# A pair's norm one unit sooner, the last w_out parts in w_in's buffers, and the first two w_in tiles in turns

## The chip, the cores and the metric

The kernel runs on one core of one Trainium2 chip. A core has a matrix engine (PE, with its weight loads shown apart as PEld), a vector engine (DVE), a scalar engine (ACT), GpSimd (POOL) and a sync engine (SP) that here issues most transfers. The metric is the time of the device for one execution, in microseconds; the kernel before took 970.9 us (median of three runs, 970.87 to 973.09). The profiled execution has a span of 971.1 us, and all times of the profile are counted from its start.

## The reference

q, k and v have the shape (8, 8, 576, 64): batch, heads, sequence, head size. The attention is linear: no softmax, one 64 x 64 matrix per head. Its normalised output is the input x of a gated MLP with 512 inputs and 2048 hidden units. The MLP's weights are float64 in memory.

```python
kv  = np.einsum('bhsd,bhse->bhde', k, v)
out = np.einsum('bhsd,bhde->bhse', q, kv)
rms = np.sqrt(np.mean(out * out, axis=-1, keepdims=True) + 1e-06)
x   = out / rms * g_norm            # -> (4608, 512)

h   = x @ w_in                      # (4608, 2048)
sp  = np.maximum(h, 0.0) + np.log1p(np.exp(-np.abs(h)))
g   = h * erf(sp)
y   = g @ w_out                     # (4608, 512)
```

## The kernel before

**Tiling.** The 4608 rows are cut into nine groups T of 512 rows. Groups 0 to 7 are the first 512 rows of each batch element; group 8 gathers the 64 rows that are left of each. The eight heads are taken as four pairs p, so one pair gives 128 of the 512 columns of x. The 2048 hidden units are 16 tiles f of 128; four tiles are a batch b. A hidden product has the shape 128 x 512 (hidden units by rows), a w_out product 128 x 512 (rows by outputs).

**A pair's attention** (`attention`, line 253) is a list of pieces that the loops place between the MLP's matmuls: `products` (kv_ps on L279, transposes of q into qt_ps on L301), `apply` (se_ps on L307, then the square on ACT, L310), `halve`, `mean` (ms_ps on L328/L329 or L333; on ACT a table load, Ln L340, Exp L341, Square L342 and a table load back), `norm` (three DVE operations, L348, L351 and L360, the last of which writes a quarter of x) and `split` (x cut into a high part on ACT, L385, and a low part and a sum of both on DVE, L388 and L389). Where the caller names no banks, kv_ps, qt_ps, se_ps and ms_ps share the two PSUM banks of `ps_at`: L348 is the last reader of ms_ps, L360 that of se_ps.

**First stage: groups 0 and 1** (loop at line 569). They are computed in plain fp32 (`h_ps`, L592, four matmuls of 128x512 over c = 0 to 3; `o_ps`, L471), one unit n for each group and f, while DVE and ACT convert the float64 weights. A conversion has three steps: `load_w`, `w_split` (L195 and L204 on DVE, L203 and L207 on ACT) and `w_join` (L214, L218, L228 on DVE). `w_order` lists the tiles by the unit at which they are due; the function `weights` does the split of the next tile, the join of the present one and the load of a later one. Four raw tiles are in memory at a time (`RAW`). The pieces of group 0's four pairs run ahead of the loop, with conversion steps between them as `w_rounds` says, and in the loop those of the next group's pairs: `pieces_of` puts the products of pair p at f = 3(p+1), its norm at f = 3(p+1)+3. A unit's work on DVE comes in this order: the norm that is due, the weights that are due, the multiplication by the erf.

**Main stage: groups 2 to 8** (loop at line 684). The weights have been cut into three parts each and stored in DRAM (`w_kept`), and `load_parts` fetches them again for each group: 768 KB a tile, w_in's into four buffers (`w_in_p`), w_out's into seven (`w_out_p`). One pass m of the loop is four hidden products of batch m (`hidden`: eight n_ps and four m_ps matmuls each, L434) and four w_out products of batch m-1 (`result`, j = 0 to 3, also twelve matmuls). `product` rotates through six banks in pairs. `FETCH` says which part is fetched at which place of a pass. Each pass also carries one pair of the next group, and the tuple `places` says after which of the eight products its pieces stand: 1 to 4 stand behind a hidden product, 5 to 8 behind a w_out product. The pieces are products, apply, halve, mean, norm, split:

```python
        places = (0, 2, 3, 5, 7, 8)
        if T + 1 == B:
            places = (0, 0, 0, 5, 7, 7)
        elif T + 2 == B and b == NB - 1:
            places = (0, 2, 3, 5, 7, 7)
```

So the norm stands behind w_out product j=2, whose two sums (L414 and L419 into e) DVE does first. Behind j=1 stands the multiplication of h by the erf (L745). [...] the order above is written out by hand (`manual_schedule`), and the tile pools add the waits for buffers.

Of the kernel before, what the change touches and what calls it, by code (L numbers as in the profile page):

```python
# [39 lines left out]
FP32 = mybir.dt.float32  # L40
# [10 lines left out]
BATCH = 4  # L51
# [7 lines left out]
def kernel(  # L59
# [11 lines left out]
    P = 128  # L71
# [3 lines left out]
    G = J * P  # L75
    R = S - G
    NP = H // 2
    KC = DM // P
    FC = DF // P
# [71 lines left out]
    w_in_sb = first_w.tile([P, KC, DF], FP32, name="w_in_sb")  # L151
# [58 lines left out]
    def w_join(which, f, k):  # L210
# [18 lines left out]


    w_order = sorted(
        [(0, "in", 0, 1), (1, "in", 1, 1)]
        + [(f, "in", f, 2) for f in range(2, FC, 2)]
        + [(min(f + LAG, (f + FC) // 2 + 1), "out", f, 2) for f in range(0, FC, 2)]
    )
    w_at = {"load": 0, "split": 0, "join": 0}
# [7 lines left out]
    def weights():  # L244

        w_next("split")
        w_next("join")
        w_next("load")
# [254 lines left out]
    for _ in range(2):  # L503
# [7 lines left out]
        2: ("join", "load", "split"),  # L511
        3: ("join", "load"),
        5: ("split",),
        6: ("join", "load"),
    }
    banks_0 = {"kv_ps": (ps_at, "at"), "qt_ps": (ps_h, "h"), "ms_ps": (ps_h, "h")}
    first = [attention(0, p, banks_0 | {"se_ps": (ps_o, f"o{p}")}) for p in range(NP)]
# [19 lines left out]

    def load_parts(which, n):

        pool = w_in_p if which == "in" else w_out_p  # L540
        for _ in range(n):
            if w_seq[which]:
                key = w_seq[which].pop(0)
                t = pool.tile([P, 3, G], FP32, name=f"w_{which}_parts", tag="w")
                nc.sync.dma_start(out=t, in_=w_kept[key])
                w_now.setdefault(key, []).append(t)


    def pieces_of(T):


        steps = [([], []) for _ in range(FC)]
        for p in range(NP):
            products, apply, halve, mean, norm, split = attention(T, p)
            short = T < FIRST or p == NP - 1
            f = (BATCH - 1) * (p + 1) if T < FIRST else BATCH * p
            steps[f][1].append(products)
            steps[f + 1][1].append(apply)
            steps[f + 2][0].append(halve)
            with_erf = short and (f + 2) % BATCH == BATCH - 1  # L560
            steps[f + 3 - short][short].append(partial(mean, table=not with_erf))
            steps[f + 4 - short][0].append(norm)
            steps[f + 5 - 2 * short][0].append(split)
        return steps

    to_cut = [(which, f) for which in ("in", "out") for f in range(FC)]
    hs, ss = {}, {}
    whole = FIRST * FC - BATCH
    for n in range(FIRST * FC + 1):
        T, f = divmod(n, FC)  # L570
        if n == FC:
            early_room.close()
            late = ctx.enter_context(tc.tile_pool(name="late", bufs=1))
            x_new = ctx.enter_context(tc.tile_pool(name="x_new", bufs=1))
            acc = ctx.enter_context(tc.tile_pool(name="acc", bufs=J))
            stage_room = ctx.enter_context(ExitStack())
            stage = stage_room.enter_context(tc.tile_pool(name="stage", bufs=5))
            x_forms[FIRST] = late.tile([P, 3, KC, G], FP32R, name="x_forms0")
        if T < FIRST:
            if f == 0:  # L580
                steps = pieces_of(T + 1)
            for piece in steps[f][0]:
                piece()
        while w_at["join"] < len(w_order) and w_order[w_at["join"]][0] <= n + 2:
            weights()
        done = n - LAG + 1
        if 0 <= done < whole:
            nc.vector.tensor_tensor(out=hs[done], in0=hs[done], in1=ss[done], op=ALU.mult)
        if T < FIRST:
            h_ps = ps_h.tile([P, G], FP32, name="h_ps", tag="h")  # L590
            for c in range(KC):
                nc.tensor.matmul(  # L592
                    h_ps,
                    lhsT=w_in_sb[:, c, f * P : f * P + P],
                    rhs=xT[T][:, c, :],
                    start=(c == 0),
                    stop=(c == KC - 1),
                )
            if n == whole:
                old_h = wide.tile([P, BATCH, G], FP32, name="h", tag="h")  # L600
            h = hs[n] = old_h[:, n - whole] if n >= whole else unit("h_sb")
            s = ss[n] = unit("s_sb")
            nc.scalar.copy(h, h_ps)
            nc.scalar.activation(s, h, AF.Softplus)
            for key in list(w_new):
                w_lower(*key)
            if T == FIRST - 1:
                for key in to_cut[:2]:
                    w_upper(*key)
                if not w_new and stage_room is not None:  # L610
                    stage_room.close()
                    stage_room = None
                    w_in_p = ctx.enter_context(tc.tile_pool(name="w_in_p", bufs=BATCH))
                    load_parts("in", BATCH)
            if n == 0:
                w_next("split")
            for piece in steps[f][1]:
                piece()
            if f % BATCH == BATCH - 1:
                for i in range(n - BATCH + 1, n + 1):  # L620
                    nc.scalar.activation(ss[i], ss[i], AF.Erf)
                softplus_table()
            if T == FIRST - 1:
                for key in to_cut[2:3]:
                    w_upper(*key)
                del to_cut[:3]
        if n >= LAG:
            T2, f2 = divmod(n - LAG, FC)
            last = n - LAG in (FC - 1, whole - 1)
            project(f2, hs[n - LAG], last)  # L630
            if last:
                sums()
                if T2 == 0:
                    for j in range(J):
                        store(T2, j, es.pop(j))
# [48 lines left out]
    for m in range(first_batch, batches + 1):  # L684
        T, b = divmod(m, NB)
        todo = []
        if T + 1 < NG:
            todo = list(attention(T + 1, b))
            if b == 0:
                side = late_r if T % 2 == FIRST % 2 else late  # L690
                x_forms[T + 1] = side.tile([P, 3, KC, G], FP32R, name=f"x_forms{(T + 1) % 2}")

        def piece():
            if todo:
                todo.pop(0)()

        places = (0, 2, 3, 5, 7, 8)
        if T + 1 == B:
            places = (0, 0, 0, 5, 7, 7)
        elif T + 2 == B and b == NB - 1:  # L700
            places = (0, 2, 3, 5, 7, 7)

        def pieces(place):
            while todo and places[-len(todo)] <= place:
                todo.pop(0)()

        def fetch(place):
            for which in FETCH[place].split():
                load_parts(which, 1)

        pieces(0)
        g, done = g_next, len(g_next)
        g_next = []
        if m < batches:
            h = wide.tile([P, BATCH, G], FP32, name="h", tag="h")
            s = gate_r.tile([P, BATCH, G], FP32, name="s", tag="s")
        for i in range(BATCH):
            if m < batches:
                n_ps, m_ps = hidden(T, b * BATCH + i)
            fetch(i)  # L720
            if i == 0:
                for half in range(done, 2):
                    g.append(cut_upper(old_h, half))
            if done <= i < 2:
                cut_lower(old_h, i, g[i])
            if m < batches:
                nc.scalar.activation(h[:, i], n_ps, AF.Copy, scale=SHIFT - 1.0)  # L727
                add(h[:, i], m_ps)
                nc.scalar.activation(s[:, i], h[:, i], AF.Softplus)  # L729
            pieces(i + 1)  # L730
        if m < batches:
            for i in range(2):
                nc.scalar.activation(part(s, i), part(s, i), AF.Erf)  # L733
            if len(todo) < 3:
                softplus_table()
        T2, b2 = divmod(m - 1, NB)
        w = [w_now["out", b2 * BATCH + f].pop(0).bitcast(FP32R) for f in range(BATCH)]
        for j in range(J):
            result(T2, b2, j, g, w)
            fetch(BATCH + j)  # L740
            if j == 1 and m == batches - 1:
                cut_lower(h, 0, g_next[0])

            for half in range(2) if j == 1 and m < batches - 1 else (j,) if j < 2 and m == batches - 1 else ():
                nc.vector.tensor_tensor(  # L745
                    out=part(h, half), in0=part(h, half), in1=part(s, half), op=ALU.mult
                )
            if j == 0 and m == batches - 1:
                g_next.append(cut_upper(h, 0))
            pieces(BATCH + 1 + j)  # L750
        old_h = h
# [33 lines left out]
```

## Time and profile before

| what | value |
|---|---|
| time, median of three runs | 970.9 us |
| span of the profiled execution | 971.1 us |
| first stage (until the main loop's first matmuls) | about 268.6 us |
| main loop, groups 2 to 6: DVE busy | 400.05 of 508 us |
| main loop, groups 2 to 6: DMA engines' share, GB/s | 0.83, 295 |
| from 34 to 60 us: DVE, ACT busy | 25.76 and 22.02 of 26 us |
| critical chain, PE's share | 81% |

In a row of the timeline stand the start, the duration, the engine and line, the operation with output and inputs, the shape and the count; in brackets the idle time before it and what released it. In a row of the page's group table stand busy time and mean duration, then the idle time ahead of the group and what ended most of it. A row such as "m_ps x4" holds four matmuls in a row. PE's start of a matmul is observed; its end is longer than the distance to the next one, since matmuls overlap.

### The profile page before, as it was taken

What the parts mean: (1) busy time and instruction counts of PE and PEld (TensorE: products, weight loads), DVE (VectorE), ACT (ScalarE), POOL (GpSimd) and SP (SyncE); (2) the same over time, 40 slices, a digit from 0 to 9 for tenths busy, and PEclk for the clock granted to TensorE, in tenths of its full rate; (3) what the DMA queues carried; (4) which work ended last, traced back from release to release, by engine and by line L of the source; (5) the groups of instructions that cost most, each with busy time, mean ns of one, the idle gap of its engine ahead of it and who ended that gap; (6) DMA issues with size and microseconds to landing.
All of it is one profiled execution on the core that took longest, in us unless ns stands there. A gap on an engine that the chain in (4) does not pass through costs nothing.

```text
span 971.1 us, 11732 instructions
## 1 busy us (share of the span) xinstructions
PE 944.2 (97%) x4328; PEld 677.5 (70%) x4328; DVE 728.4 (75%) x1031; ACT 615.2 (63%) x821; POOL 2.4 (0%) x10
## 2 busy tenths in 40 slices
PE   6899999999999999999999999999999999999997
PEld 4344444444477877787778777877887787878885
DVE  3987866766377777887787778877777777887666
ACT  3888865686576666666666666666666666665551
POOL 0000000000000000000000000000000000000000
PEclk9999999999999999999999999999999999999999
DMA  9855506879289975998789877987796669767852
GB/s 281 246 177 178 179 1 272 311 320 361 95 293 352 378 272 210 306 367 295 247 270 357 305 274 243 350 290 294 247 335 254 259 228 363 275 261 295 351 231 76
DMA packets 100937, 259.76 MB, mean 267 GB/s; under 512 B 44049, under 2 KB 57361, under 8 KB 100881
## 3 DMA queue, kind: packets, MB, share of 16 engines
q1 hardware_dynamic: 99248, 256.73, 74.0%
q10 hardware_dynamic: 1568, 2.29, 0.8%
q8 instruction: 34, 0.56, 0.2%
q14 instruction: 23, 0.18, 0.1%
q0 software_dynamic: 64, 0.00, 0.0%
HBM read 224.40 MB, written 34.60 MB: 267 GB/s over the span
## 4 chain that ended last, share of the span: by engine, by line
PE 81%; DVE 12%; ACT 4%; DMA 2%; issue 1%; SPq 0%; DVEq 0%
PE n_ps L434 35%; PE m_ps L434 18%; PE h_ps L592 10%; PE o_ps L471 9%; PE se_ps L307 3%; DVE h L745 3%; DVE e L419 2%; PE qt_ps L301 2%; PE kv_ps L279 2%; DMA w_out_parts<-w_out 1%; DVE x L360 1%; DVE e L414 1%; DVE u L351 1%; DVE u L348 1%; PE ms_ps L328 1%
## 5 line engine op out<-in xcount | busy, mean ns | idle before, releaser
L434 PE MATMUL n_ps<-x_forms,w_in_parts 128*128 128x512 f32 x896 | 233.3, 402 | 1.7 <-ACT x_forms L385 1.2
L434 PE MATMUL n_ps<-w_out_parts,g_forms 128*128 128x512 f32 x928 | 231.8, 391 | 2.5 <-DMA w_out_parts<-w_out 2.5
L434 PEld LDWEIGHTS n_ps<-w_out_parts,g_forms 128*128 128x128 f32 x928 | 174.1, 188 | 41.7 <-DMA w_out_parts<-w_out 3.4
L434 PEld LDWEIGHTS n_ps<-x_forms,w_in_parts 128*128 128x128 f32 x896 | 166.8, 188 | 45.8 <-issue 9.6
L729 ACT ACTIVATE s<-h 128x512 f32<-128x512 f32 x112 | 71.0, 634 | 168.0 <-DVE h L419 168.0
L434 PE MATMUL m_ps<-w_out_parts,g_forms 128*128 128x512 f32 x464 | 124.2, 389 | 0.0
L434 PE MATMUL m_ps<-x_forms,w_in_parts 128*128 128x512 f32 x448 | 120.1, 390 | 0.0
L419 DVE TENSOR_TENSOR h<-m_ps,h 128x512 f32<-128x512 f32 x112 | 77.1, 688 | 56.9 <-ACT h L727 41.5
L592 PE MATMUL h_ps<-xT,w_in_sb 128*128 128x512 f32 x256 | 116.7, 600 | 2.9 <-DVE xT L360 2.0
L471 PE MATMUL o_ps<-w_out_sb,h_sb 128*128 128x512 f32 x224 | 100.5, 592 | 0.0
L434 PEld LDWEIGHTS m_ps<-w_out_parts,g_forms 128*128 128x128 f32 x464 | 87.1, 188 | 18.1
L414 DVE SCALAR_TENSOR_TENSOR e<-n_ps,e 128x512 f32<-128x512 f32 x88 | 60.5, 687 | 49.2 <-PE n_ps L434 49.2
L434 PEld LDWEIGHTS m_ps<-x_forms,w_in_parts 128*128 128x128 f32 x448 | 84.1, 188 | 17.6
L419 DVE TENSOR_TENSOR e<-m_ps,e 128x512 f32<-128x512 f32 x116 | 80.3, 692 | 18.5 <-PE m_ps L434 12.2
L592 PEld LDWEIGHTS h_ps<-xT,w_in_sb 128*128 128x128 f32 x256 | 49.0, 192 | 64.3 <-issue 58.0
L471 PEld LDWEIGHTS o_ps<-w_out_sb,h_sb 128*128 128x128 f32 x224 | 42.0, 190 | 49.8 <-issue 48.3
L389 DVE SCALAR_TENSOR_TENSOR g_forms<-g_forms 128x1024 fp32r<-128x1024 f32 x58 | 71.1, 1225 | 2.0
L388 DVE TENSOR_TENSOR g_forms<-h,g_forms 128x1024 fp32r<-128x1024 f32 x58 | 70.6, 1218 | 1.5 <-ACT g_forms L385 1.2
L727 ACT ACTIVATE h<-n_ps 128x512 f32<-128x512 f32 x112 | 65.5, 585 | 4.1 <-PE n_ps L434 4.1
L385 ACT ACTIVATE g_forms<-h 128x1024 fp32r<-128x1024 f32 x58 | 58.9, 1059 | 13.8 <-PE m_ps L434 11.0
L745 DVE TENSOR_TENSOR h<-h,s 128x1024 f32<-128x1024 f32 x56 | 66.0, 1219 | 0.4 <-ACT s L733 0.4
L385 ACT ACTIVATE x_forms<-x 128x512 fp32r<-128x512 f32 x28 | 17.7, 631 | 66.8 <-DVE x L360 66.8
(84 smaller groups left out, 981.2 us busy)
## 6 DMA issues: line engine op xcount, KB each, us to landing
w_out_parts<-w_out SPq DMA_DIRECT2D x116, 768.0 KB, 7.6
w_in_parts<-w_in SPq DMA_DIRECT2D x112, 768.0 KB, 6.6
w_in<-w_new SPq DMA_DIRECT2D x16, 768.0 KB, 5.6
w_out<-w_new SPq DMA_DIRECT2D x16, 768.0 KB, 6.4
k_sb<-in_k_dram SPq DMA_DIRECT2D x29, 288.0 KB, 5.6
v_sb<-in_v_dram SPq DMA_DIRECT2D x29, 288.0 KB, 5.5
q_sb<-in_q_dram SPq DMA_DIRECT2D x32, 256.0 KB, 5.6
w_raw<-in_moe_w_out_dram SPq DMA_DIRECT2D x8, 1024.0 KB, 5.0
```

The lines of the kernel that those rows point to most:

```text
L307: nc.tensor.matmul(o_ps, lhsT=bd, rhs=qT, start=True, stop=True)
L385: nc.scalar.activation(high, x, AF.Copy, scale=1.0 + 2.0**-13)
L388: nc.vector.tensor_tensor(out=low, in0=x, in1=high.bitcast(FP32), op=ALU.subtract)
L389: nc.vector.scalar_tensor_tensor(out=both, in0=low.bitcast(FP32), scalar=SHIFT, in1=high.bitcast(FP32), op0=ALU.mult, op1=ALU.add,)
L414: nc.vector.scalar_tensor_tensor(out=out_, in0=ps, scalar=scale, in1=out_, op0=ALU.mult, op1=ALU.add)
L419: nc.vector.tensor_tensor(out=out_, in0=ps, in1=out_, op=ALU.add)
L434: nc.tensor.matmul(ps, lhsT=weights(form, k), rhs=moving(form, k), start=(form == forms[0] and k == 0), stop=(form == forms[-1] and k == 3),)
L471: nc.tensor.matmul(o_ps[j], lhsT=g[:, j * P : j * P + P], rhs=w_out_sb[:, f, :], start=(f == 0), stop=last,)
L592: nc.tensor.matmul(h_ps, lhsT=w_in_sb[:, c, f * P : f * P + P], rhs=xT[T][:, c, :], start=(c == 0), stop=(c == KC - 1),)
L727: nc.scalar.activation(h[:, i], n_ps, AF.Copy, scale=SHIFT - 1.0)
L729: nc.scalar.activation(s[:, i], h[:, i], AF.Softplus)
L745: nc.vector.tensor_tensor(out=part(h, half), in0=part(h, half), in1=part(s, half), op=ALU.mult)
```

## The change

It has four parts. In the main loop a pair's norm moves from place 7 to place 6, ahead of the sums of w_out product j=2. The last four w_out parts are fetched into w_in's buffers, which are no longer needed then, so that they don't have to wait for w_out buffers that are still read. In the first stage, where two weight tiles are due in one unit, one is converted ahead of the unit's pieces. And the first two w_in tiles take the blocks c of x in turns (tile 0 and tile 1 with c=0, then both with c=1, and so on), in banks of other pools, so that the PE has more to do while the last pair of x is computed; the w_in tiles up to f=3 are converted one by one instead of in twos for it.

```diff
     w_order = sorted(
-        [(0, "in", 0, 1), (1, "in", 1, 1)]
-        + [(f, "in", f, 2) for f in range(2, FC, 2)]
+        [(f, "in", f, 1) for f in range(4)]
+        + [(f, "in", f, 2) for f in range(4, FC, 2)]
         + [(min(f + LAG, (f + FC) // 2 + 1), "out", f, 2) for f in range(0, FC, 2)]
     )
...
-        6: ("join", "load"),
+        6: ("split", "join", "load", "join", "load"),
     }
...
     def load_parts(which, n):

-        pool = w_in_p if which == "in" else w_out_p
+
+        pool = w_out_p if which == "out" and len(w_seq["out"]) > BATCH else w_in_p
...
+    def due(k):
+
+        i = w_at["join"] + k
+        return i < len(w_order) and w_order[i][0] <= n + 2
+
     for n in range(FIRST * FC + 1):
...
+            if due(1):
+                weights()
             for piece in steps[f][0]:
                 piece()
-        while w_at["join"] < len(w_order) and w_order[w_at["join"]][0] <= n + 2:
+        while due(0):
             weights()
...
         if T < FIRST:
-            h_ps = ps_h.tile([P, G], FP32, name="h_ps", tag="h")
-            for c in range(KC):
+
+            if n > 1:
+                plain[n] = ps_h.tile([P, G], FP32, name="h_ps", tag="h")
+                blocks = [(n, c) for c in range(KC)]
+            elif n == 0:
+                for i, (pool, tag) in enumerate(((ps_at, "at"), (ps_o, "o0"))):
+                    plain[i] = pool.tile([P, G], FP32, name="h_ps", tag=tag)
+                blocks = [(i, c) for c in range(KC - 1) for i in range(2)] + [(0, KC - 1)]
+            else:
+                blocks = [(1, KC - 1)]
+            for i, c in blocks:
                 nc.tensor.matmul(
-                    h_ps,
-                    lhsT=w_in_sb[:, c, f * P : f * P + P],
+                    plain[i],
+                    lhsT=w_in_sb[:, c, i % FC * P : i % FC * P + P],
                     rhs=xT[T][:, c, :],
                     start=(c == 0),
                     stop=(c == KC - 1),
                 )
+            h_ps = plain.pop(n)
...
-        places = (0, 2, 3, 5, 7, 8)
+
+        places = (0, 2, 3, 5, 6, 8)
         if T + 1 == B:
-            places = (0, 0, 0, 5, 7, 7)
+            places = (0, 0, 0, 5, 6, 7)
         elif T + 2 == B and b == NB - 1:
-            places = (0, 2, 3, 5, 7, 7)
+            places = (0, 2, 3, 5, 6, 7)
```

More of the change, by code (lines that the diff above doesn't have):

```diff
@@ L566 @@
     to_cut = [(which, f) for which in ("in", "out") for f in range(FC)]
-    hs, ss = {}, {}
+    hs, ss, plain = {}, {}, {}
     whole = FIRST * FC - BATCH
+    def due(k):
+        i = w_at["join"] + k
+        return i < len(w_order) and w_order[i][0] <= n + 2
     for n in range(FIRST * FC + 1):
```

## The prediction

> **What bounds the kernel now.** I read the engine totals first, then the PE's idle gaps in order of time, and only then the other engines around each gap. Totals and the largest PE row of the page:
>
> ```profile
> PE 944.2 (97%) x4328; PEld 677.5 (70%) x4328; DVE 728.4 (75%) x1031; ACT 615.2 (63%) x821; POOL 2.4 (0%) x10
> L434 PE MATMUL n_ps<-x_forms,w_in_parts 128*128 128x512 f32 x896 | 233.3, 402 | 1.7 <-ACT x_forms L385 1.2
> ```
>
> The PE is the bound: of 971.1 us only 27 are not busy, so each part of the change is worth the PE gap it closes. The ends of PE records are modelled, so I measure a gap by distances between starts, not by the bracketed idle time (eight n_ps matmuls advance 1.81 us, the four m_ps ones 0.91, eight fp32 ones 3.43). The PE timeline holds these gaps, all that matter:
>
> ```profile
> 29.31 2.84 PE L592 MATMUL h_ps<-xT,w_in_sb 128*128 128x512 f32 x6 [0.94 <-DVE qT L348]
> 34.14 13.12 PE L592 MATMUL h_ps<-xT,w_in_sb 128*128 128x512 f32 x26 [1.98 <-DVE xT L360]
> ...
> 58.01 1.12 PE L333 MATMUL ms_ps<-qT,mean_w 128*128 128x512 f32 x2 [1.25 <-ACT qT L310]
> ...
> 123.84 0.43 PE L306 MATMUL kv_ps<-qT_last,bd_kv 128*128 128x64 f32 x2 [1.48 <-DVE bd_kv L294]
> ...
> 343.94 0.92 PE L279 MATMUL kv_ps<-v_sb,k_sb 96*64 96x64 f32 x24
> 345.13 0.66 PE L301 MATMUL qt_ps<-ident,q_sb 128*128 128x128 f32 x4 [0.27 <-DVE x L360]
> ...
> 774.02 0.49 PE L434 MATMUL n_ps<-x_forms,w_in_parts 128*128 128x512 f32 x1 [0.42 <-ACT x_forms L385]
> ...
> 956.82 0.72 PE L434 MATMUL n_ps<-w_out_parts,g_forms 128*128 128x512 f32 x2 [2.06 <-DMA w_out_parts<-w_out]
> 957.38 1.09 PE L434 MATMUL m_ps<-w_out_parts,g_forms 128*128 128x512 f32 x4
> ```
>
> The reader is to see five kinds: the start, one wait on ACT at 58, one on DVE at 124, a small one that recurs at every seam between two batches, and the last w_out part.
>
> [...] the four-matmul gap doubles from 34.14, where the clock record has 3.41 us at 0.5 and the 3.41 us before were busy for only 1.4. [...]
>
> **Part 1, the norm at place 6 instead of 7 (main loop).** Nothing is added; three DVE operations move ahead of the two sums of w_out product j=2. One seam of before, from the DVE and ACT timelines:
>
> ```profile
> 340.23 0.63 ACT L342 ACTIVATE u<-rms_r 128x512 f32<-128x512 f32 x1
> 341.49 0.68 DVE L414 SCALAR_TENSOR_TENSOR e<-n_ps,e 128x512 f32<-128x512 f32 x1
> 342.28 0.69 DVE L419 TENSOR_TENSOR e<-m_ps,e 128x512 f32<-128x512 f32 x1
> 342.88 0.68 DVE L348 SCALAR_TENSOR_TENSOR u<-ms_ps,u 128x512 f32<-128x512 f32 x1
> 343.60 0.69 DVE L351 SCALAR_TENSOR_TENSOR u<-u,rms_r 128x512 f32<-128x512 f32 x1
> 344.33 0.75 DVE L360 SCALAR_TENSOR_TENSOR x<-se_ps,gm_col,u 128x512 f32<-128x512 f32 x1
> ```
>
> The next pair's kv_ps takes the bank that L348 frees (342.88+0.68 = 343.56, and the PE's loads start only then), its qt_ps the bank that L360 frees (345.08). Put first, the norm would start at 341.5: u is ready at 340.86, 0.6 us before, so no wait is put in its place. L360 then ends at 343.7, before kv_ps begins. The sums of j=2 end 2.1 us later, near 345.0; their banks are next wanted by hidden unit 1 at 348.4. The sums of j=3 keep their time, since DVE does the same work without a gap.
>
> Price: the batches that start with odd p advance 25.21 us from kv_ps to kv_ps, those with even p 25.16. Free of waits, from the first batch at 268.6 (24.96, less 0.09 at its end), they would take 24.70 and 24.87 (the odd lack one transpose of 0.17). So 0.51 and 0.29 each. Ten odd ones give 5.0. Of nine even ones, five give 1.45. The other four open a new group T: there the low third of x (L388) still comes after j=3's sums at an unchanged time (372.27 at the first such seam, where the PE would want it at 372.0), so I leave them 0.09 each, 0.35. Sum **6.8**. The ends: 0 if those waits return elsewhere, 8.0 if all nineteen are won.
>
> Two seams without products. At 772.08 the PE takes 3.01 us to the m_ps at 775.09 instead of 1.81; with norm and split each a unit sooner, L388 would end near 773.9 where 773.67 is wanted: 0.95 of the 1.2 is won. At 864.62 the loss is 1.55, and there ACT's L342 ends only at 863.96, so the norm can't start sooner; j=2's sums now stand between it and L388, which ends 0.6 later. In the group before, the new order lets DVE wait for ACT (up to 1.7 us a batch), in others it saves 0.45, so I take **-0.4** (ends 0 and -1.5). Net +0.55.
>
> **Part 2, the last four w_out parts in w_in's buffers.** The stop at 956.82 costs 957.38-953.24-1.81 = 2.33 us: of seven w_out buffers four are read until 953, so the eighth transfer starts then and lands after the row's
>
> ```profile
> 952.75 4.03 DMA w_out_parts<-w_out
> ```
>
> of the critical chain. The four w_in buffers come free with the last hidden units, 934 to 942.4, so all four parts land near 950 at the 7.6 us from issue to landing that the page has. Nothing else waits in that queue but stores that come later. The work then met is DVE's L389 (ends 958.5), wanted by j=2 only at about 960.5. **+2.3** (ends 1.5, 2.4).
>
> **Part 3, conversion ahead of the norm where two are due.** That happens in unit n=12 only. DVE there waited 3.73 us for ACT (L342, until 110.95), and was then late with bd_kv at 123.34. With 4.8 us of conversion put into that wait the norm begins at 112.0, one us later, and bd_kv is done near 121.4; the PE wants it at 122.36. The gap of **1.5** goes (ends 0, 1.5).
>
> **Part 4, the first two tiles in turns, w_in in single tiles to f=3.** The PE's 0.94 at 29.31 goes (h_ps leaves ps_h, whose bank waited for L348) and the 1.98 at 34.14 is filled: six blocks of 0.86 from 28.15, the seventh when the last xT comes (about 33.5, since a shorter split stands before it). But DVE has no gap from 30 to 60, so converting the tiles sets what follows. Two single joins of 1.93 take 0.33 more than one double (34.00 to 37.53), and the split for f=4 moves from 37.53 to about 37.95. ACT, held by it at 38.25 (1.3 us idle), goes from 38.7; it then wins back the 0.69 that it waited for the PE at units 2, 3 and qt_ps, and reaches
>
> ```profile
> 57.38 0.58 ACT L310 ACTIVATE qT<-se_ps 128x512 f32<-128x512 f32 x1
> ```
>
> 0.25 us sooner. That L310 releases the ms_ps at 58.01, behind which all later PE work queues. So of the PE's four us only **+0.25** arrives; the rest becomes idle time before 57.8, some 3.6 us in one piece (units 4 and 5 done at 54.15). [...] I take **-1.1**. Net -0.85 (ends -1.5 and +4, if ACT isn't the limit).
>
> The stop at 808.81 (0.75 by starts) I leave as it is, +-0.5.
>
> **Sum.** 6.8+0.55+2.3+1.5-0.85 = 10.3; 970.9-10.3 = **960.6**.
>
> **The rivals.** (a) The seams keep half: L388 or the banks stop the PE a little later than now. For: DVE is 79% busy from 264 to 772 (400 of 508 us). Against: it waits 2.6 us a batch for the PE. 6.8 becomes 3: about 964.4. Chance 0.17. (b) The start is won in full (+4 instead of -0.85): 955.8. Against it stands the gapless DVE. 0.08. (c) Transfers become the limit once batches are shorter, and the seam gap turns into one for parts: only 2.3+1.5-0.85 and 0.55 remain, 967.4. Against: the DMA engines are at 83%, and parts are waited for in two places only. 0.05. (d) The norm blocks DVE on u in most batches, holding j=2's banks: if each of 28 batches lost 0.2 us instead of gaining, with part 4 at -1.5, parts 2 and 3 at 2.3 and 0: 970.9+5.6+1.5-2.3 = 975.7, slower. Against: 0.6 us of slack on u. 0.04. The forecast keeps 0.66.
>
> **Range.** The forecast's unknown ends (part 4, new groups, the 808 stop) span about 957.5 to 963; (a) reaches 965. So 957.2 to 965.0, leaving out (b) to (d) and some tail. Faster by over 0.3% means under 968.0: the forecast, (a), (b) and most of (c), 0.94; same 0.02; slower 0.04.
>
> **What would show it.** Right: no qt_ps row with a wait for L360 in the main loop, odd batches at 24.7 us and even at 24.9; waits for x_forms at new groups; no stop at the last w_out part; none at unit 13; L360 no longer before h_ps at the start, but a longer wait for L310 before ms_ps and perhaps a half-clock window after it. Wrong: DVE idle before L348 for u in batches before 772, or ms_ps near 54.

## The result, and the profile after

The changed kernel takes 966.34 us (median of four runs, 965.56 to 966.64) beside 972.0 us for the kernel before on the same chip: a ratio of 0.9939 with a 95% interval of 0.9918 to 0.9959, 5.9 us of 972. That is the direction of the forecast, but a little over half of its 10.3 us, and 1.3 us above the end of its range. The profiled span went from 971.1 to 964.5 us.

The page's totals and the row of the hidden products, after:

```profile
PE 942.4 (98%) x4328; PEld 677.5 (70%) x4328; DVE 727.9 (75%) x1036; ACT 615.4 (64%) x823; POOL 2.4 (0%) x10
L434 PE MATMUL n_ps<-x_forms,w_in_parts 128*128 128x512 f32 x896 | 234.1, 402 | 2.4 <-ACT x_forms L385 1.4
```

The PE is still the bound, but the idle time ahead of the hidden products has grown from 1.7 to 2.4 us. Nearly all of it stands at group 8's start (1.42 and 0.83 us, below), where a loss of 0.4 us was forecast. The PE timeline, with the places of before (start, duration, operation, idle time before it and who ended it):

```profile
28.11 7.38 PE L610 MATMUL h_ps<-xT,w_in_sb 128*128 128x512 f32 x16
36.10 7.13 PE L610 MATMUL h_ps<-xT,w_in_sb 128*128 128x512 f32 x16 [0.61 <-DVE w_in_sb L228]
...
49.51 0.44 PE L306 MATMUL kv_ps<-qT_last,bd_kv 128*128 128x64 f32 x2 [1.30 <-DVE qT_last L297]
...
57.14 2.07 PE L333 MATMUL ms_ps<-qT,mean_w 128*128 128x512 f32 x2 [2.85 <-ACT qT L310]
59.01 5.74 PE L471 MATMUL o_ps<-w_out_sb,h_sb 128*128 128x512 f32 x8
64.59 3.60 PE L610 MATMUL h_ps<-xT,w_in_sb 128*128 128x512 f32 x8
...
124.40 0.33 PE L306 MATMUL kv_ps<-qT_last,bd_kv 128*128 128x64 f32 x2
...
342.81 1.07 PE L434 MATMUL m_ps<-w_out_parts,g_forms 128*128 128x512 f32 x4
343.81 0.92 PE L279 MATMUL kv_ps<-v_sb,k_sb 96*64 96x64 f32 x24
344.66 0.66 PE L301 MATMUL qt_ps<-ident,q_sb 128*128 128x128 f32 x4
345.08 2.10 PE L434 MATMUL n_ps<-x_forms,w_in_parts 128*128 128x512 f32 x8
...
859.25 1.52 PE L434 MATMUL n_ps<-x_forms,w_in_parts 128*128 128x512 f32 x6
862.18 0.50 PE L434 MATMUL n_ps<-x_forms,w_in_parts 128*128 128x512 f32 x1 [1.42 <-ACT x_forms L385]
863.52 0.51 PE L434 MATMUL n_ps<-x_forms,w_in_parts 128*128 128x512 f32 x1 [0.83 <-DVE x_forms L388]
863.86 1.07 PE L434 MATMUL m_ps<-x_forms,w_in_parts 128*128 128x512 f32 x4
...
949.09 1.98 PE L434 MATMUL n_ps<-w_out_parts,g_forms 128*128 128x512 f32 x8
950.90 1.07 PE L434 MATMUL m_ps<-w_out_parts,g_forms 128*128 128x512 f32 x4
```

What the reader is to see: the two stops at the start of h_ps are down to one of 0.61 (a new one of 1.30 stands at 49.51), and none is left at unit 13 (124.40), at qt_ps or at the last w_out part (949.09). But behind the wait at 57.14 eight o_ps matmuls take 5.6 us from start to start where they took 3.43, and the first product of group 8 (859.25) takes 4.61 us to its m_ps, against 3.36 before and 1.81 when nothing stops it.

Split into stages by the starts of kv_ps, before and after: up to the main loop 268.61 and 269.06 (0.45 later); the main loop from there to the last pair's kv_ps 478.40 and 474.18 (4.22 won); from there to the end 224.1 and 221.3 (2.8 won). The last is made of 2.33 at the last w_out part, 0.79 at group 7's start (3.01 becomes 2.22), 0.75 at the stop of 808, which isn't there in this run, and -1.25 at group 8's start; 0.2 are left over, the last pair's own seam among them. The 0.75 is luck: no part of the change aims at that stop.

### The profile page after: what moved, and what is told of

Same layout as the page of the kernel before. It is cut to its first block, busy times and chain, and to the rows that moved or that the text cites. A ratio compares the mean times of both kernels' runs of the same rounds, so it can differ in the third digit from the quotient of the medians.

```text
span 964.5 us, 11755 instructions
## 1 busy us (share of the span) xinstructions
PE 942.4 (98%) x4328; PEld 677.5 (70%) x4328; DVE 727.9 (75%) x1036; ACT 615.4 (64%) x823; POOL 2.4 (0%) x10
## 4 chain that ended last, share of the span: by engine, by line
PE 84%; DVE 6%; ACT 6%; DMA 1%; issue 1%; SPq 0%; DVEq 0%
PE n_ps L434 37%; PE m_ps L434 19%; PE o_ps L471 10%; PE h_ps L610 9%; PE se_ps L307 3%; PE kv_ps L279 2%; PE qt_ps L301 1%; DVE h L419 1%; ACT s L753 1%; DMA v_sb<-in_v_dram 1%; ACT s L749 1%; DVE e L419 1%; DVE g_forms L388 1%; DMA q_last<-in_q_dram 1%; PE ms_ps L328 1%
## 5 line engine op out<-in xcount | busy, mean ns | idle before, releaser
L471 PE MATMUL o_ps<-w_out_sb,h_sb 128*128 128x512 f32 x224 | 102.7, 603 | 0.0
L414 DVE SCALAR_TENSOR_TENSOR e<-n_ps,e 128x512 f32<-128x512 f32 x88 | 60.4, 686 | 44.1 <-PE n_ps L434 44.1
L388 DVE TENSOR_TENSOR g_forms<-h,g_forms 128x1024 fp32r<-128x1024 f32 x58 | 70.6, 1218 | 1.5 <-ACT g_forms L385 1.2
```

The costliest lines, as they stand in the source:

```text
L388: nc.vector.tensor_tensor(out=low, in0=x, in1=high.bitcast(FP32), op=ALU.subtract)
L414: nc.vector.scalar_tensor_tensor(out=out_, in0=ps, scalar=scale, in1=out_, op0=ALU.mult, op1=ALU.add)
L471: nc.tensor.matmul(o_ps[j], lhsT=g[:, j * P : j * P + P], rhs=w_out_sb[:, f, :], start=(f == 0), stop=last,)
```

## The experiments

Two theories stood against each other for the first stage. Theory C (clock): part 4 moves idle time into one piece ahead of ms_ps, and the PE then runs the work behind it at half clock. Rival: the start's gain is real, and the loss lies elsewhere. For group 8's start: the norm's place against ACT's lateness. Each time below is given with the kernel before on the same chip.

**e1: without part 4.**

```diff
-        [(f, "in", f, 1) for f in range(4)]
-        + [(f, "in", f, 2) for f in range(4, FC, 2)]
+        [(0, "in", 0, 1), (1, "in", 1, 1)]
+        + [(f, "in", f, 2) for f in range(2, FC, 2)]
...
-        6: ("split", "join", "load", "join", "load"),
+        6: ("join", "load"),
...
-            if n > 1:
-                plain[n] = ps_h.tile([P, G], FP32, name="h_ps", tag="h")
-                blocks = [(n, c) for c in range(KC)]
...
-            for i, c in blocks:
+            h_ps = ps_h.tile([P, G], FP32, name="h_ps", tag="h")
+            for c in range(KC):
```

> The changed kernel without part 4 (no turns, w_in tiles in twos as before); parts 1 to 3 stay. Theory: part 4 costs about 2 us, since the PE, idle before the ms_ps of group 1's first pair, falls to half clock [...]. Then this kernel has no half-clock stretch after 57 us, keeps part 3's 1.5 us, and takes 8 to 8.5 us less than before, 2.5 us less than the changed kernel. Rival: the start's gain is real and the loss lies elsewhere; then this kernel is 0.9 us slower than the changed one, about 4.8 us less than before.

Measured: 964.25 us beside 972.25, ratio 0.9918 (0.9902 to 0.9933), 8.0 us less. The main loop begins at 265.25 instead of 269.06; 0.28 of that is an earlier start of this run (the last ms_ps of group 0 is at 26.89, in the changed kernel at 27.17). So without part 4 the first stage is 3.5 us shorter, more than the 2 us of the expectation: ms_ps comes at 56.39, 29.50 us behind that last ms_ps of group 0, and in the changed kernel 29.97. Against this run part 4 did not even bring it forward. In the profiled run of before the distance was 30.74; the section on the prediction comes back to this. The end of e1 gave something back, though. The stretches of e1 around group 8's start (columns: stretch, length, busy time and instructions of PE, PEld, DVE, ACT and POOL, granted PE clock, share of the DMA engines, GB/s):

```profile
857.00:861.00 4.00, 1.65 (x5) 0.87 (x4) 3.83 (x6) 3.01 (x4) 0.00 (x0) 0.85 0.48 187
861.00:868.00 7.00, 7.00 (x21) 5.45 (x20) 6.83 (x9) 1.83 (x3) 0.00 (x0) 0.60 0.31 112
```

There the stop for x_forms (1.52 and 0.83 us) leaves the PE busy for 1.65 of 4 us, and the clock is at half from 859.78 to 866.61: the same kind of fall at another place.

**e2: part 4 alone** (the norm's places and the pool for w_out as before, no conversion ahead of the unit's pieces).

> The kernel before with part 4 alone. Theory: ms_ps starts 0.9 us sooner (57.1), then half clock costs about 3.1 us, so the PE is some 2.1 us late at unit 13, where DVE's lateness (the 1.48 us wait for bd_kv) is now covered: the main loop begins 0.5 to 1.0 us later than before, time +0.5 to +1.0 us. Rival, the clock isn't the cause: -0.9 us.

Measured: 974.13 us beside 972.25, ratio 1.0019 (1.0011 to 1.0027): 1.8 us slower. The sign is Theory C's, the size larger (the interval, 1.1 to 2.6 us, lies above the expected 0.5 to 1.0). In its trace ms_ps starts at 57.16, the clock from 57 to 64 is 0.76 (in the changed kernel 0.55), and the wait for bd_kv in unit 13 is still 1.44 us: DVE's lateness moved along with the PE, so nothing was covered. That part of the expectation was wrong.

**e3: unit 5 done twice in the changed kernel.**

```diff
+            if n == LAG:
+                blocks = blocks * 2
             for i, c in blocks:
```

> The changed kernel with the four h_ps matmuls of unit 5 done twice (the second time over the first): 3.4 us of PE work more, put into the idle time before ms_ps. Theory of the clock: ms_ps starts near 57.6 instead of 57.1, but at full rate, and the stretch to unit 6 takes 4.4 us instead of 7.5: 2.6 us less than the changed kernel, 8 to 8.5 us less than before, although it computes more. Rival, the slow stretch has another cause (data, banks, DMA): 0.4 us slower than the changed kernel.

Measured: 964.25 us beside 972.25, ratio 0.9923 (0.9906 to 0.9939): 7.5 us less than before with 3.4 us of PE work more. The stretches of the changed kernel and of e3:

```profile
57.00:64.00 7.00, 6.86 (x9) 2.91 (x10) 3.66 (x5) 6.86 (x10) 0.00 (x0) 0.55 0.50 181
```

```profile
58.00:65.00 7.00, 7.00 (x18) 3.09 (x17) 3.69 (x5) 6.86 (x9) 0.00 (x0) 1.00 0.48 163
```

In seven microseconds the PE did 9 instructions at a clock of 0.55, and 18 at full clock; from ms_ps to unit 6 the first takes 7.45 us, the second 4.29. The two kernels differ in the repeated matmuls alone, which fill the PE's idle time. This shows Theory C for the first stage. The time moves with the clock from run to run, too: three of e3's six runs have a mean clock of 1.000 and take 962.94 to 963.26 us, the other three 0.998 and 965.23 to 967.16. The profiled one is of the second kind, with half clock behind group 8's start (861.64 to 865.06).

**e4: the first w_out product ahead of ms_ps in the changed kernel.**

```diff
+            if n == LAG:
+                project(0, hs[0], False)
             for piece in steps[f][1]:
                 piece()
...
-        if n >= LAG:
+        if n > LAG:
```

> The changed kernel with the first w_out product (unit 0's, eight fp32 matmuls, 3.43 us) ahead of the ms_ps of group 1's first pair instead of behind it. Theory: the idle 2.85 us are filled with work that has to be done anyway, the clock stays full, and the PE reaches unit 6 near 59.1 instead of 64.6: about 5 us less than the changed kernel at that point; of it 1 us may be lost to the pair's norm, which starts 1 us later on DVE: 9.5 to 10.5 us less than before. Rival, DVE and ACT set the time there: 1 us or less is won against the changed kernel.

Measured: 964.5 us beside 972.25, ratio 0.9919 (0.9905 to 0.9933): 7.9 us less, where 9.5 to 10.5 was expected. Unit 6 starts at 58.75, but then the pair's norm is waited for, as the rival had it in part:

```profile
57.89 1.02 PE L333 MATMUL ms_ps<-qT,mean_w 128*128 128x512 f32 x2
58.75 3.60 PE L610 MATMUL h_ps<-xT,w_in_sb 128*128 128x512 f32 x8
63.80 0.92 PE L279 MATMUL kv_ps<-v_sb,k_sb 96*64 96x64 f32 x24 [1.46 <-DVE qT L348]
65.32 0.66 PE L301 MATMUL qt_ps<-ident,q_sb 128*128 128x128 f32 x4 [0.59 <-DVE xT L360]
```

Unit 6 comes 5.8 us sooner than in the changed kernel, 0.5 of it by an earlier start (26.68 against 27.17 for the last ms_ps of group 0); 2.05 of the rest come back as this wait, and the main loop begins at 265.40. Part of the shortfall goes with the clock: the two runs at a mean clock of 1.000, the profiled one among them, take 962.57 and 963.32 us, the four at 0.998 or 0.996 take 964.39 to 965.47.

**e5: the norm of group 8's pairs back at place 7.**

```diff
         if T + 1 == B:
-            places = (0, 0, 0, 5, 6, 7)
+            places = (0, 0, 0, 5, 7, 7)
```

> The changed kernel, with the norm of group 8's pairs back at place 7 (the tuple for T + 1 == B is (0, 0, 0, 5, 7, 7) again). Theory: at place 6 DVE waits there for ACT's L342 and then does two sums before L388, so the first product of group 8 comes 2.8 us late instead of 1.55, [...]. Then that stop is 1.3 us shorter, no half-clock stretch follows it, and the time is 1.3 to 3 us less than the changed kernel's, 7 to 9 us less than before. Rival: ACT's lateness is what counts there, and the place doesn't matter: within 0.5 us of the changed kernel.

Measured: 963.38 us beside 972.63, ratio 0.9912 (0.9899 to 0.9924): 8.6 us less, inside the expected 7 to 9. In its trace the first product of group 8 takes 857.33 to 860.85, 3.52 us, with a stop of 0.93 for ACT and 0.23 for DVE, and the clock stays at 1.00 from 857 to 868. The place matters: 1.09 us less than the 4.61 of the changed kernel. The rest of the difference between the two includes the clock near 57, at half for 3.41 us in this run and for 6.83 in the other: from ms_ps to unit 6 it is 6.09 us against 7.45.

**e6: part 1 alone.**

> The kernel before with part 1 alone (norm at place 6). Theory from the seams counted again: odd batches 24.84 instead of 25.21 us, even ones 24.96 instead of 25.16, those that open a group unchanged: 4.3 us up to the last of them, then +0.8 at group 7's start and -1.25 (more with the half clock) at group 8's: 3.0 to 4.5 us less than before. Rival, as predicted: 6.8 and 0.55, 7.3 us less.

Measured: 969.08 us beside 972.63, ratio 0.997 (0.9961 to 0.9978), 2.9 us less. That is just under the expected 3.0 to 4.5, and far from the rival's 7.3. The seams are as in the changed kernel (24.84 and 24.96 us, 25.2 where a group opens). What else it shows is the spread: 22 runs from 967.2 to 972.8 us, and the profiled one is the slowest. Its stretches behind the stop at group 8's start and behind the last w_out part:

```profile
864.00:868.00 4.00, 4.00 (x11) 3.19 (x12) 3.86 (x5) 0.99 (x2) 0.00 (x0) 0.59 0.13 15
...
956.00:960.00 4.00, 4.00 (x12) 3.11 (x12) 1.66 (x3) 0.00 (x0) 0.00 (x0) 0.57 0.21 52
```

Both stops were followed by half clock in this execution, and in the profiled run of the kernel before neither was (1.00 from 868 to 872 and from 957 to 961). Each costs up to 1.7 us, an estimate: half of the 3.41 us that the clock record has at half.

**e7: part 2 alone.**

> The kernel before with part 2 alone (last four w_out parts in w_in's buffers). Theory: the stop of 2.3 us at the last w_out product goes, and in runs where that stop is followed by half clock up to 1.7 us more: 2.0 to 3.5 us less than before. Rival, the end is set by DVE's forms or the stores: under 1 us.

Measured: 968.73 us beside 972.63, ratio 0.997 (0.996 to 0.9981), 2.9 us less, with an interval of 1.8 to 3.9: the stop's 2.3, and perhaps some of the clock behind it. Of the four profiled kernels that keep this stop, e2 and e6 show a clock of 0.57 over four microseconds behind it, e9 shows four m_ps matmuls in 1.71 us instead of 0.91, and before shows 1.00. There is no stop left in e7's last products.

**e8: parts 1 to 3 with two places mended.** To e1 come e5's edit and

```diff
-        elif T + 2 == B and b == NB - 1:
+        elif b == NB - 1:
             places = (0, 2, 3, 5, 6, 7)
```

> Without part 4, with parts 1 to 3, and two places mended: norm at place 7 for group 8's pairs, and at each last batch of a group the split at place 7 instead of 8, ahead of j=3's sums. Theory: against the kernel without part 4 (8 us less than before) the four seams that open groups 3 to 6 win 0.2 to 0.35 us each, 1.1 us, and group 8's start 1.3 us and its half clock: 10.5 to 12 us less than before, faster than both kernels. Rival for the seams: L388 is held by ACT or x, and they stay at 25.2 us.

Measured: 961.94 us beside 972.63, ratio 0.9892 (0.9876 to 0.9907), 10.5 us less. One seam that opens a group, in the changed kernel on DVE, then in e8 on DVE and on the PE:

```profile
370.49 0.69 DVE L419 TENSOR_TENSOR e<-m_ps,e 128x512 f32<-128x512 f32 x1
371.10 0.68 DVE L388 TENSOR_TENSOR x_forms<-x,x_forms 128x512 fp32r<-128x512 f32 x1
```

```profile
367.31 0.68 DVE L388 TENSOR_TENSOR x_forms<-x,x_forms 128x512 fp32r<-128x512 f32 x1
368.02 0.69 DVE L389 SCALAR_TENSOR_TENSOR x_forms<-x_forms 128x512 fp32r<-128x512 f32 x1
368.63 0.68 DVE L414 SCALAR_TENSOR_TENSOR e<-n_ps,e 128x512 f32<-128x512 f32 x1
...
367.63 2.10 PE L434 MATMUL n_ps<-x_forms,w_in_parts 128*128 128x512 f32 x8
369.57 1.07 PE L434 MATMUL m_ps<-x_forms,w_in_parts 128*128 128x512 f32 x4
```

In the changed kernel L388 ends at 371.78, 1.76 us after n_ps has begun (370.02), which then takes 2.16 us to its m_ps; in e8 it ends at 367.99, and n_ps takes 1.94. All batches that open a group become 24.96 us instead of 25.2.

**e9: part 3 alone.**

> The kernel before with part 3 alone (one weight tile ahead of the norm in unit 12). Theory, as predicted: the wait for bd_kv in unit 13 goes, the PE gains 1.5 us there and keeps it: 1.5 us less than before. Rival: the wait is passed on to a later unit (the norm comes 1 us later): 0.5 us or less.

Measured: 972.12 us beside 973.05, ratio 0.9989 (0.998 to 0.9997), 1.1 us less. The wait in unit 13 is gone (kv_ps follows unit 13's h_ps at 122.04 without a stop, bd_kv is written at 120.93), and it isn't passed on: from unit 6 to the main loop the profiled runs that have part 3 and o_ps in its old place take 204.5 us, those without part 3 206.2. In this run the stop near 808 is 1.64 us by its idle time, 0.47 in the first run of before; over the runs of this study it goes from none to 1.64, and I have no cause for that.

**e10: the changed kernel without part 3.**

```diff
-            if due(1):
-                weights()
```

> The changed kernel without part 3. If the gains of parts 3 and 4 add, it is 1.5 us slower than the changed kernel. Theory: with part 4 the PE comes to unit 13 about 2 us late; the run with part 4 alone still showed a wait of 1.44 us for bd_kv there, so DVE's lateness moves along with the PE (its chain begins with the norm, which waits for ACT and so for the PE's ms_ps), and the two parts add: 1.2 to 1.6 us slower than the changed kernel, about 5 us less than before. Rival: covered, within 0.3 us of the changed kernel.

Measured: 967.75 us beside 973.05, ratio 0.9942 (0.993 to 0.9955), 5.6 us less. The trace has the wait for bd_kv back (1.49 us at 125.83), and from unit 6 to the main loop it takes 206.22 us against 204.47 in the changed kernel, so the parts do add there. The times can't tell: this run was at half clock for 3.41 us near 58 and the changed kernel for 6.83, which makes 1.4 us between ms_ps and unit 6 (6.09 against 7.45). By time the run is inconclusive.

**e11: e8's mended places, with part 4 and e4's edit.**

> The mended kernel (norm and split as in e8) with part 4 kept and the first w_out product put ahead of ms_ps. Theory: the main loop begins near 265.4 as in e4, against 266.7 in e8, and all seams are as in e8: 1 us less than e8, 11.5 us less than before. Rival: the wait for the pair's norm at 63.8 (1.46 and 0.59 us in e4) takes it back: equal to e8 within 0.5 us.

Measured: 960.96 us beside 973.05, ratio 0.988 (0.9864 to 0.9896), 11.7 us less: the fastest kernel of the study by its median. Its main loop begins at 266.18, e8's at 266.66; the interval overlaps with e8's, so whether part 4 is worth keeping once the PE is kept busy stays open.

## Why the prediction was wrong

It was wrong in size. In the profiled pair 6.6 us are won of the 10.3: the seams bring 2.6 less than forecast, part 4 costs 1.4 more (2.3: 0.77 won and 3.06 lost, both below) and group 8's start 0.85 more, while the stop of 808 gave 0.75 that was not in the forecast. The parts alone (e6, e7, e9 and e2) add up to 5.1 us, the whole to 5.9, so, as far as their intervals tell, the shortfall lies within the parts and not in how they act together. By the runs:

**The seams (6.8 forecast, 4.2 measured).** The mechanism held: qt_ps waits for L360 no more, the norm begins at once behind the multiplication by the erf (L348 at 341.36, with L414 of j=2 behind it at 343.47), no wait for u took its place, L388 held the seams that open a group. The step that failed is the price of a seam free of waits. I took 0.09 us ahead of kv_ps off the 24.96 us of the first batch, as a wait for L348, and left 0.06 behind qt_ps out. Neither is a wait. In all 19 seams kv_ps starts 1.00 us after the m_ps ahead of it (0.91 between products), before, when L348 ended 0.38 us ahead of kv_ps, and after, when it ended 1.77 us ahead. At the main loop's first kv_ps (269.06), 7.3 us behind the last norm, sixteen o_ps matmuls take 6.96 us instead of twice 3.43, the same 0.09 more. From qt_ps to n_ps the changed kernel takes 0.41 to 0.42 us in odd batches and 0.36 in even ones. So odd batches are 24.84 at best, not 24.70, and even ones 24.96, not 24.87. Ten by 0.37 and five by 0.20 are 4.7, less 0.37 for the last seam, which lies outside the stage, and less than 0.1 that the four opening seams lost. (In the forecast's own sum ten times 0.51 is 5.1, not 5.0, and all nineteen seams would be 7.7, not 8.0.)

**Part 4 (a loss of 0.85 us forecast, 1.8 measured by e2).** The reasoning by DVE held: the split for f=4 came at 37.89 (37.95 forecast), and L310 set ms_ps. Two steps failed, both on the clock. The first is that ACT "wins back the 0.69 that it waited for the PE". Those waits were there because the PE ran at half clock from 34.73 to 38.14 in that run of before, and I had taken this stretch to be hidden. ACT's way from the split for f=4 (L203) to L310 takes 19.13 us there, 17.90 in the changed kernel and 17.89 in e1, which has neither part 4 nor half clock in that stretch: 1.23 us, not 0.69, and none of it due to part 4. The distance from the last ms_ps of group 0 to the ms_ps after unit 5 tells it:

| kernels | part 4 | where the start ran at half clock | distance, us |
|---|---|---|---|
| before, e8, e9 | no | behind the stop at h_ps (34 us) | 30.74 |
| e1 | no | not from 26 to 41 us | 29.50 |
| e6, e7 | no | earlier, in the first h_ps matmuls (e6: 0.66 from 31 to 36 us; e7: six of them take 4.47 us instead of 2.84) | 29.49, 29.50 |
| after, e2, e5, e10 | yes | not from 26 to 41 us | 29.95 to 29.97 |

Against a run with that stretch part 4 wins 0.77 us, more than the 0.25 forecast; against one without it loses 0.47, which is the later split that I had worked out at 0.42. The second step, which turned this into the larger loss, is the size of the half clock behind ms_ps. The forecast's 1.1 us was my estimate from the one stretch of before, 3.41 us at half; at this place before ran at 1.00 (58 to 64 us). It took 3.06 (7.45 against 4.39 us from ms_ps to unit 6): the clock record of this run has 6.83 us at half, from 56.49 on; in e2, e5 and e10 it has 3.41, and the cost is 1.70. So part 4 has no single price. Among the profiled kernels with part 3 and nothing further new in the first stage, the main loop begins 238.4 us behind the last ms_ps of group 0 in e1 and 239.6 in e8 and e9, all without part 4; with it 240.5 in e5 and 241.9 in the changed kernel.

**Group 8's start (-0.4 forecast, -1.25 measured).** The step "L388 ends 0.6 later" left out that ACT itself comes later: L342 ended at 859.23, level with the first n_ps, where before it ended 0.66 us ahead of its n_ps, and in e5, with the norm back at place 7, 0.50 ahead. DVE's waits for L342 ahead of the norms of group 8's four pairs grow from 0.25 to 0.75, 1.53 and 1.91 us; before has 0.26 at the last pair alone, e5 0.24 and 0.42 at the last two. The last of the changed kernel:

```profile
859.26 0.69 DVE L348 SCALAR_TENSOR_TENSOR sq<-ms_ps,sq 128x512 f32<-128x512 f32 x1 [1.91 <-ACT sq L342]
```

The stop grew from 1.55 to 2.80 us. Beyond that I had counted no half clock behind this stop. There is some in the profiled runs of e1 and e3 (a clock of 0.60 and 0.76 from 861 to 868) and of e6 (0.59 from 864 to 868), none in that of the changed kernel (1.00 from 864 to 872).

**Right:** group 7's start (0.95 forecast, 0.79), part 2 (2.3, 2.33), part 3 (1.5 forecast, 1.7 in e9's and e10's traces), and the list of what would be seen, but for the two lengths of a batch. Of the rivals, (c) has the nearest time (967.4), but the PE waits for no part in the changed kernel's main loop, so its mechanism did not come true. (a) has the nearest size at the seams (3 us), for a reason that it didn't name: no wait returned at the ordinary seams; less had been there to win.

## What to carry to other kernels

Before a gap is priced as a wait, look at the same seam where nothing can be waited for: here kv_ps came 1.00 us after m_ps with no wait in it, where two products are 0.91 apart. Where idle time is moved rather than removed, price the place that it goes to: gathered into one piece of 2.85 us ahead of ms_ps, it was followed by a loss of 3.06 us at half clock, where the start had won 0.77. Work that has to be done anyway can be put into it: e4 did so, and unit 6 began at 58.75 instead of 64.59, though e4 came out no faster than e1, which leaves part 4 out. Where one engine's order is changed for all passes of a loop, check the passes whose inputs come at other times; here the same move of the norm won 4.2 us in groups 2 to 6 and lost 1.25 at group 8's start.

## What the runs showed of the hardware

The PE's granted clock fell behind some stops and not behind others. Stops of the profiled runs, with the PE's busy time in a stretch that holds the stop, and the granted clock in the stretch behind it:

| run | stretch with the stop, us | PE busy, us | stretch behind, us | granted clock there |
|---|---|---|---|---|
| before | 30 to 34 | 2.15 of 4 | 34 to 38 | 0.59 |
| e1 | 31 to 36 | 3.02 of 5 | 36 to 41 | 1.00 |
| changed kernel | 50 to 57 | 4.29 of 7 | 57 to 64 | 0.55 |
| e5 | 50 to 57 | 4.21 of 7 | 57 to 64 | 0.76 |
| e1 | 857 to 861 | 1.65 of 4 | 861 to 868 | 0.60 |
| e3 | 857 to 861 | 1.66 of 4 | 861 to 868 | 0.76 |
| changed kernel | 860 to 864 | 1.75 of 4 | 864 to 868 | 1.00 |
| e2 | 955 to 959 | 1.65 of 4 | 959 to 963 | 0.57 |
| e6 | 952 to 956 | 1.58 of 4 | 956 to 960 | 0.57 |
| before | 953 to 957 | 1.94 of 4 | 957 to 961 | 1.00 |

The clock was at half for 3.41 us in before (from 34.73), in e3 (from 861.64) and in e5 (from 56.89), and for 6.83 us in e1 (from 859.78) and in the changed kernel (from 56.49). The changed kernel and e5 have the same program up to there, and nearly the same busy time ahead. Why one lost twice as much as the other, and why one of two like stops was followed by full clock, the runs did not show; none was made for that. The busy times rest on modelled ends.

The half-clock stretch of before at 34 us, in a stage where DVE has no gap, moved ms_ps by 1.24 us (30.74 against 29.50): ACT sat between the two. So the price of these stops changed from run to run. That fits the spread of e6's 22 runs: the two at a mean clock of 0.994 take 971.85 and 972.78 us, the two at 0.998 take 967.18 and 969.13. Not all of that spread goes with the clock: the seven runs at 0.995 lie between 968.65 and 971.05.
